# Joining the half-empty row tails of two batches in the second product of an attention and MLP kernel, with fewer buffers elsewhere

## The chip, the cores and the metric

The kernel runs on one core of one Trainium2 chip. The metric is the device time of one execution in microseconds (us), as a median of several.

Names: PE (TensorE) does the matmuls, PEld its weight loads, DVE (VectorE) and ACT (ScalarE) move and transform results, POOL issues the loads with a type cast, SP issues the stores. "L406" is line 406 of that version's file. Line numbers shift from version to version; tile names do not, except that `ch1T` is called `ch1Tp` after the change.

## The reference

```python
# q, k, v: (8 batches, 8 heads, 576 rows, 64); causal attention with a window of 64
x = softmax(mask(q @ k.T / 8)) @ v            # heads joined: (8, 576, 512)
u = x + ((x.transpose(0, 2, 1) @ U) @ V).transpose(0, 2, 1)      # U, V: rank 32
out = u + relu(u @ w_ch1) @ w_ch2             # w_ch1: 512x2048, w_ch2: 2048x512
```

A batch has 576 rows: four chunks of 128 and a tail of 64.

## The kernel before

The kernel interleaves two jobs: the MLP of batch b and the attention of batch b+1. The attention needs `v` in two alignments: `vaugA` is loaded, and `vaugB` is the same data moved by 64 rows, which DVE copies from `vaugA`. The kernel is written with a layer that orders each engine's instructions itself, allots buffers and sets all semaphores. The order on an engine is therefore not simply that of the source, and the number of buffers helps to decide it.

```python
ld_pool  = tc.tile_pool(name="ld",  bufs=3)      # q, k
va_pool  = tc.tile_pool(name="va",  bufs=3)      # vaugA and vaugB: three buffers each
ch1_pool = tc.tile_pool(name="ch1", bufs=1)
out_pool = tc.tile_pool(name="osb", bufs=6)
ps_big   = tc.tile_pool(name="ps_big", bufs=2, space=PSUM)   # shared by psA, psU, pshh
# ...
        vaugB = va_pool.tile([P, NFULL, H, VW], BF16, name="vaugB")
        def prep():
            nc.vector.memset(vaugA[:, :, :, D:VW], 1.0)
            nc.vector.tensor_copy(out=vaugB[0:W, 0:NFULL, :, :], in_=vaugA[W:P, 0:NFULL, :, :])
            nc.vector.tensor_copy(out=vaugB[W:P, 0:NFULL, :, :], in_=vaugA[0:W, 1:NC, :, :])
# ... the second product, one chunk t of rows
        def make_ch2(t):
            def f():
                mt = P if t < NFULL else REM          # 128, and 64 for the tail
                psU = ps_big.tile([P, 512], FP32, name="psU", tag="big")
                for i in range(NFC):                  # 16
                    nc.tensor.matmul(psU[0:mt, :], ch1T[:, i, t * P : t * P + mt], w2b[:, i, :],
                                     start=(i == 0), stop=(i == NFC - 1))
                osb = out_pool.tile([P, DM], FP32, name="osb")
                nc.vector.tensor_tensor(out=osb[0:mt, :], in0=psU[0:mt, :],
                                        in1=u_b16[0:mt, t, :], op=ALU.add)
                nc.sync.dma_start(out=out[b, t * P : t * P + mt, :], in_=osb[0:mt, :])
# ... the main loop
    for b in range(B):
        if b + 2 < B:
            loads(b + 2)
        mlp = mlp_phases(b, holders.pop(b))
        # emit_interleaved(attention of b + 1, mlp of b); the last batch has its MLP alone
```

The softmax here doesn't subtract the row's maximum and nothing guards it: scores larger than these inputs give would overflow.

## Time and profile before

| | before |
|---|---|
| median time | 435.55 us (434.36 to 436.71, 6 runs) |
| span of the profiled run | 433.6 us |
| PE busy | 88% of the span |
| second product (psU) in the chain of waits | 30% of the span |

The page first: the busy shares, and the TensorE clock that was granted, in tenths, over 40 equal slices.

```profile
PE 383.1 (88%) x3034; PEld 199.1 (46%) x3088; DVE 229.2 (53%) x622; ACT 137.1 (32%) x361; POOL 109.5 (25%) x134
...
PEclk9965897999996999989999999999999999999999
```

PE is the busiest engine by far (88%, the next 53%) and holds 67% of the chain of waits, so what lengthens PE's work, or stops it, costs time. The clock row shows dips below 9 in the first 45% of the span and none later. Something happens there that later batches do not have.

To find it, read the chain that ended last in order of time and pick a fixed point of each batch: the start of its third full chunk of psU. The columns are start, length, what, and how many.

```profile
88.13 3.40 PE psU L406 x15
92.09 7.02 PE psU L406 x32
...
140.28 3.40 PE psU L406 x15
...
192.09 3.40 PE psU L406 x15
...
243.18 3.40 PE psU L406 x15
...
290.57 3.45 PE psU L406 x16
...
338.02 3.45 PE psU L406 x16
...
385.47 3.45 PE psU L406 x16
```

The differences are 52.15, 51.81, 51.09, 47.39, 47.45 and 47.45 us. The same work takes about 4.3 us longer in the first three. (The line at 92.09 us is the fourth full chunk and the tail of batch 0 together.) The VectorE timeline of the first slow batch shows why: start, length, instruction, and in brackets how long the engine sat idle before it and what ended that.

```profile
125.06 0.42 DVE L282 TENSOR_TENSOR x_b<-xr,rcp 64x256 bf16<-64x256 f32 x1
130.41 0.76 DVE L164 COPY vaugB<-vaugA 64x2304 bf16<-64x2304 bf16 x1 [4.93 <-DMA vaugA<-in_v_dram]
131.19 0.69 DVE L414 TENSOR_TENSOR osb<-psU,u_b 128x512 f32<-128x512 f32 x1
```

The copy at 130.41 us is for batch 5, whose attention is three batches ahead. With three `vaugB` buffers there is a free one, so the copy stands in DVE's queue just behind the load that it needs, and DVE waits for the transfer. The urgent instruction, `osb`, which empties a PSUM buffer that PE needs, stands behind the copy. In this trace DVE ran nothing past the waiting copy: psU was complete at about 128.6 us, and `osb` starts only at 131.19 us, right behind the copy. The next two batches show the same order (copies at 183.01 and 234.10 us after 5.39 and 4.67 us of idle time, `osb` at 183.79 and 234.88 us). PE's timeline and its clock in the same stretch (columns of the second fence: stretch, its length, busy us of each engine, granted clock, DMA share, GB/s):

```profile
128.42 0.38 PE L318 MATMUL psA<-hhTb,vmoe 128*128 128x512 bf16 x1
131.94 1.18 PE L318 MATMUL psA<-hhTb,vmoe 128*128 128x512 bf16 x2 [3.14 <-DVE osb L414]
```

```profile
124.00:129.00 5.00, 4.62 (x23) 1.86 (x24) 1.36 (x6) 0.58 (x1) 3.21 (x4) 1.00 1.60 105
129.00:134.00 5.00, 2.05 (x7) 0.71 (x6) 3.41 (x6) 0.00 (x0) 0.00 (x0) 0.72 0.40 69
134.00:139.00 5.00, 5.00 (x17) 1.94 (x17) 2.05 (x3) 0.00 (x0) 0.00 (x0) 0.60 0.00 0
139.00:144.00 5.00, 4.95 (x33) 2.64 (x33) 0.97 (x2) 1.31 (x5) 0.00 (x0) 1.00 0.14 52
```

PE stands still for 3.14 us and then runs at a mean granted clock of 0.60 from 134 to 139 us: the chunk of 16 psU matmuls that starts at 134.78 us takes 5.2 us, where the 16 at 290.57 us, in a batch without a stall, take 3.45. The stall is paid twice. Its sums over the whole kernel, in the view of waits (us in total, times, longest):

```profile
DVE vaugB L164 <- DMA vaugA<-in_v_dram: 23.3, 7, 5.4
...
PE psA L318 <- DVE osb L414: 11.9, 7, 3.6
...
PE psB L382 <- DVE x_b L282: 3.5, 1, 3.5
```

The last line belongs to the first batch. There the copy stands ahead of an attention result (`x_b`) instead of `osb`, and PE waits for that; after this wait its granted clock is 0.50 from 71 to 76 us:

```profile
68.47 0.76 DVE L164 COPY vaugB<-vaugA 64x2304 bf16<-64x2304 bf16 x1 [3.51 <-DMA vaugA<-in_v_dram]
```

The other two stalls show it too: after PE gaps of 3.60 and 2.88 us the granted clock is 0.50 from 186 to 188 us and from 237 to 240 us. From 255 us to the end, where no wait of PE is longer than 0.6 us, its mean is 1.00. Beyond this sequence, nothing here shows what ties the clock to the gap.

### The profile page before, as it was taken

What the parts mean: (1) busy time and instruction counts of PE and PEld (TensorE: products, weight loads), DVE (VectorE), ACT (ScalarE), POOL (GpSimd) and SP (SyncE); (2) the same over time, 40 slices, a digit from 0 to 9 for tenths busy, and PEclk for the clock granted to TensorE, in tenths of its full rate; (3) what the DMA queues carried; (4) which work ended last, traced back from release to release, by engine and by line L of the source; (5) the groups of instructions that cost most, each with busy time, mean ns of one, the idle gap of its engine ahead of it and who ended that gap; (6) DMA issues with size and microseconds to landing.
All of it is one profiled execution on the core that took longest, in us unless ns stands there. A gap on an engine that the chain in (4) does not pass through costs nothing.

```text
span 433.6 us, 7457 instructions
## 1 busy us (share of the span) xinstructions
PE 383.1 (88%) x3034; PEld 199.1 (46%) x3088; DVE 229.2 (53%) x622; ACT 137.1 (32%) x361; POOL 109.5 (25%) x134
## 2 busy tenths in 40 slices
PE   0647996899988999699996999999998999999996
PEld 0433652346533565245642455445643465444542
DVE  5376774636745187443775257642775167532321
ACT  1331751026510174113720236212830255221300
POOL 9929459933430052300703000000000000000000
PEclk9965897999996999989999999999999999999999
DMA  8999999994980179811949110011000110011011
GB/s 56 147 194 137 178 153 135 153 139 58 91 56 24 73 60 64 57 48 60 80 33 80 48 39 2 2 48 49 13 2 26 49 39 2 2 48 62 0 50 61
DMA packets 121042, 28.35 MB, mean 65 GB/s; under 512 B 113808, under 2 KB 115888, under 8 KB 121008
## 3 DMA queue, kind: packets, MB, share of 16 engines
q0 software_dynamic: 115760, 18.43, 57.4%
q1 hardware_dynamic: 5248, 9.44, 6.1%
q8 instruction: 24, 0.39, 0.4%
q14 instruction: 10, 0.08, 0.1%
HBM read 36.85 MB, written 9.44 MB: 107 GB/s over the span
## 4 chain that ended last, share of the span: by engine, by line
PE 67%; DMA 12%; POOL 8%; DVE 5%; ACT 5%; issue 2%; DVEq 0%; POOLq 0%
PE psU L406 30%; PE psA L374 19%; DMA vaugA<-in_v_dram 5%; POOL vaugA L143 4%; DMA w2b<-in_moe_w_ch_dram 4%; PE xr L273 3%; DMA w1b<-in_moe_w_ch_dram 3%; PE psB L382 3%; ACT ptj L236 3%; PE sc L228 3%; DVE u_b L325 2%; POOL qb L137 2%; POOL kb L133 2%; PE tp L191 2%; PE tp L340 2%
## 5 line engine op out<-in xcount | busy, mean ns | idle before, releaser
L406 PE MATMUL psU<-w2b,ch1T 128*128 128x512 bf16 (+1 forms) x628 | 148.2, 387 | 1.0 <-DVE ch1T L393 0.5
L374 PE MATMUL psA<-uT,w1b 128*128 128x512 bf16 x474 | 134.0, 383 | 2.4 <-ACT uT L348 0.6
L406 PEld LDWEIGHTS <-ch1T 128*128 128x128 bf16 (+1 forms) x640 | 63.1, 102 | 72.9 <-issue 11.0
L414 DVE TENSOR_TENSOR osb<-psU,u_b 128x512 f32<-128x512 f32 (+1 forms) x40 | 27.6, 690 | 107.1 <-PE psU L406 107.0
L390 ACT ACTIVATE ch1T<-psA 128x512 bf16<-128x512 f32 x64 | 38.2, 597 | 65.2 <-PE psA L374 61.0
L133 POOL DMA_DIRECT2D kb<-in_k_dram x40 | 36.9, 923 | 81.2 <-PE tp L178 72.3
L374 PEld LDWEIGHTS <-w1b 128*128 128x128 bf16 x512 | 42.3, 98 | 23.0 <-issue 0.8
L393 DVE TENSOR_SCALAR ch1T<-psA 128x512 bf16<-128x512 f32 x64 | 44.1, 689 | 13.3 <-PE psA L374 10.1
L348 ACT COPY uT<-tp 128x512 bf16<-128x512 bf16 x32 | 19.0, 594 | 94.6 <-PE tp L343 94.6
L236 ACT ACTIVATE ptj<-sc 128x384 bf16<-128x384 f32 x96 | 43.9, 495 | 6.6 <-PE sc L228 4.9
L382 PEld LDWEIGHTS <-w1b 128*128 128x128 bf16 x512 | 31.2, 99 | 24.8 <-DVE x_b L282 4.0
L143 POOL DMA_DIRECT2D vaugA<-in_v_dram x40 | 33.8, 886 | 30.2 <-PE psA L374 30.2
L382 PE MATMUL psB<-uT,w1b 128*128 128x64 bf16 x512 | 37.0, 195 | 4.6 <-DVE x_b L282 3.5
L137 POOL DMA_DIRECT2D qb<-in_q_dram x40 | 36.2, 904 | 9.6 <-DMA w2b<-in_moe_w_ch_dram 9.6
L183 ACT COPY kt<-tp 128x512 bf16<-128x512 bf16 x32 | 18.8, 588 | 58.6 <-PE tp L178 58.5
L242 DVE TENSOR_TENSOR ptj<-ptj,maskall 128x384 bf16<-128x384 bf16 x96 | 31.3, 353 | 10.5 <-ACT ptj L236 9.2
L203 DVE COPY qbd<-tp 64x512 bf16<-64x512 bf16 x64 | 26.9, 421 | 17.1 <-PE tp L196 16.4
L282 DVE TENSOR_TENSOR x_b<-xr,rcp 128x256 bf16<-128x256 f32 (+1 forms) x80 | 32.9, 415 | 1.4
L273 PEld LDWEIGHTS <-ptj 128*64 128x64 bf16 x576 | 18.3, 116 | 30.8 <-DVE x_b L282 13.9
L228 PE MATMUL sc<-qbd,kt 128*128 128x128 bf16 x288 | 29.4, 224 | 3.4 <-DVE qbd L203 1.5
L318 PE MATMUL psA<-hhTb,vmoe 128*128 128x512 bf16 (+1 forms) x40 | 17.7, 447 | 15.4 <-DVE osb L414 11.9
L228 PEld LDWEIGHTS <-kt 128*128 128x128 bf16 x288 | 20.7, 100 | 14.0 <-issue 8.5
(48 smaller groups left out, 295.0 us busy)
## 6 DMA issues: line engine op xcount, KB each, us to landing
out_dram<-osb SPq DMA_DIRECT2D x32, 256.0 KB, 2.0
kb<-in_k_dram POOLq DMA_DIRECT2D x32, 128.0 KB, 4.5
qb<-in_q_dram POOLq DMA_DIRECT2D x32, 128.0 KB, 4.6
vaugA<-in_v_dram POOLq DMA_DIRECT2D x32, 128.0 KB, 4.5
w1b<-in_moe_w_ch_dram POOLq DMA_DIRECT2D x1, 2048.0 KB, 14.4
w2b<-in_moe_w_ch_dram POOLq DMA_DIRECT2D x1, 2048.0 KB, 16.9
out_dram<-osb SPq DMA_DIRECT2D x8, 128.0 KB, 2.2
kb<-in_k_dram POOLq DMA_DIRECT2D x8, 64.0 KB, 4.0
```

The lines of the kernel that those rows point to most:

```text
L133: nc.gpsimd.dma_start(out=kb16[0:rows, c, :, :], in_=k[b, :, c * P : c * P + rows, :].rearrange("h p d -> p h d"),)
L137: nc.gpsimd.dma_start(out=qb16[0:rows, c, :, :], in_=q[b, :, c * P : c * P + rows, :].rearrange("h p d -> p h d"),)
L143: nc.gpsimd.dma_start(out=vaugA[0:rows, c, :, 0:D], in_=v[b, :, c * P : c * P + rows, :].rearrange("h p d -> p h d"),)
L228: nc.tensor.matmul(sc[:, bb, :], kt[:, j, w0 : w0 + P], qbd[:, j, blk, :, :].rearrange("p g q -> p (g q)"), start=True, stop=True,)
L236: nc.scalar.activation(out=ptj[:, prange, :, :], in_=sc[:], func=ACT.Exp, scale=scale,)
L273: nc.tensor.matmul(xr[r0 : r0 + W, hl, 0 : D + 1], pts[j][:, blk, g, :], rhs, start=True, stop=True,)
L282: nc.vector.tensor_tensor(out=x_b16[0:mt, t, 4 * hh : 4 * hh + 4, :], in0=xr[0:mt, :, 0:D], in1=rcp[0:mt, :, :].to_broadcast([mt, 4, D]), ...
L374: nc.tensor.matmul(psA[:, :], w1b[:, dc, i * P : (i + 1) * P], uT[:, dc, 0:512], start=(dc == 0), stop=(dc == NDC - 1),)
L382: nc.tensor.matmul(psB[:, :], w1b[:, dc, i * P : (i + 1) * P], uT[:, dc, 512:S], start=(dc == 0), stop=(dc == NDC - 1),)
L390: nc.scalar.activation(out=ch1T[:, i, 0:512], in_=psA[:, :], func=ACT.Relu)
L393: nc.vector.tensor_relu(out=ch1T[:, i, 0:512], in_=psA[:, :])
L406: nc.tensor.matmul(psU[0:mt, :], ch1T[:, i, t * P : t * P + mt], w2b[:, i, :], start=(i == 0), stop=(i == NFC - 1),)
```

## The change

The intent: the tail of a batch fills 64 of the 128 rows of a psU result, yet its 16 matmuls take as long as those of a full chunk (a full chunk and a tail take 7.02 us, a full chunk alone 3.45). The change keeps the first layer's results of two batches in one tile, places the two tails side by side, and computes both with one chunk of 128 rows when the odd batch is done. It also takes buffers away elsewhere, presumably to make room for the doubled tile. From the shapes, `ch1Tp` takes 36 KB per partition instead of 18 KB; the buffers given up are two of 5 KB (q, k), one `vaugA` of 5.6 KB, two `vaugB` of 4.5 KB and two `osb` of 2 KB.

```diff
-    ld_pool = ...(name="ld", bufs=3)
-    va_pool = ...(name="va", bufs=3)
+    ld_pool = ...(name="ld", bufs=2)
+    va_pool = ...(name="va", bufs=2)
+    ut_pool = ...(name="ut", bufs=2)
+    vb_pool = ...(name="vb", bufs=1)
-    out_pool = ...(name="osb", bufs=6)
+    out_pool = ...(name="osb", bufs=4)
-        vaugB = va_pool.tile(...)
+        vaugB = vb_pool.tile(...)
-        ch1T = ch1_pool.tile([P, NFC, S], BF16, name="ch1T")
+        even = b % 2 == 0
+        if even:
+            ch1Tp = ch1_pool.tile([P, NFC, 2 * S], BF16, name="ch1Tp")
+            colb, colt = 0, 512              # columns of the chunks, and of the tail
+            utail = ut_pool.tile([P, DM], BF16, name="utail")
+            nc.scalar.copy(out=utail[0:REM, :], in_=u_b16[0:REM, NFULL, :])
+        else:                                # same ch1Tp and utail as the even batch
+            colb, colt = S + REM, S          # this tail stands next to the even one's
+            nc.scalar.copy(out=utail[REM:P, :], in_=u_b16[0:REM, NFULL, :])
         # ... the first layer writes ch1Tp at colb and colt
+        # chunks of an even batch: its four full ones. Of an odd batch: its four full ones,
+        # then one of 128 rows at column 512 (both tails), residual utail, two stores
-                nc.sync.dma_start(out=out[b, t * P : t * P + mt, :], in_=osb[0:mt, :])
+                for (bb, s0, s1), orows in stores:
+                    nc.sync.dma_start(out=out[bb, s0:s1, :], in_=osb[orows, :])
```

More of the change, by code (lines that the diff above doesn't have):

```diff
@@ L52 @@
     qbd_pool = ctx.enter_context(tc.tile_pool(name="qbd", bufs=1))
-    ld_pool = ctx.enter_context(tc.tile_pool(name="ld", bufs=3))
-    va_pool = ctx.enter_context(tc.tile_pool(name="va", bufs=3))
+    ld_pool = ctx.enter_context(tc.tile_pool(name="ld", bufs=2))
+    va_pool = ctx.enter_context(tc.tile_pool(name="va", bufs=2))
+    ut_pool = ctx.enter_context(tc.tile_pool(name="ut", bufs=2))
+    vb_pool = ctx.enter_context(tc.tile_pool(name="vb", bufs=1))
     kt_pool = ctx.enter_context(tc.tile_pool(name="kt", bufs=2))
@@ L59 @@
     wk_pool = ctx.enter_context(tc.tile_pool(name="wk", bufs=4))
-    out_pool = ctx.enter_context(tc.tile_pool(name="osb", bufs=6))
+    out_pool = ctx.enter_context(tc.tile_pool(name="osb", bufs=4))
     ps_sc = ctx.enter_context(tc.tile_pool(name="ps_sc", bufs=2, space=bass.MemoryType.PSUM))
@@ L125 @@
     loaded = {}
+    pair_state = {}
     def loads(b):
@@ L159, in attention_phases @@
         kt = kt_pool.tile([P, HP, S], BF16, name="kt")
-        vaugB = va_pool.tile([P, NFULL, H, VW], BF16, name="vaugB")
+        vaugB = vb_pool.tile([P, NFULL, H, VW], BF16, name="vaugB")
         def prep():
@@ L366, in mlp_phases @@
         phases = []
-        ch1T = ch1_pool.tile([P, NFC, S], BF16, name="ch1T")
+        even = b % 2 == 0
+        partner_missing = even and (b + 1 >= B)
+        if even:
+            ch1Tp = ch1_pool.tile([P, NFC, 2 * S], BF16, name="ch1Tp")
+            pair_state["tile"] = ch1Tp
+            pair_state["u_even"] = u_b16
+            colb = 0
+            colt = 512
+            utail = ut_pool.tile([P, DM], BF16, name="utail")
+            pair_state["utail"] = utail
+            nc.scalar.copy(out=utail[0:REM, :], in_=u_b16[0:REM, NFULL, :])
+        else:
+            ch1Tp = pair_state["tile"]
+            colb = S + REM
+            colt = S
+            utail = pair_state["utail"]
+            nc.scalar.copy(out=utail[REM:P, :], in_=u_b16[0:REM, NFULL, :])
         def make_ch1(i):
@@ L389, in f @@
                 if i % 2 == 0:
-                    nc.scalar.activation(out=ch1T[:, i, 0:512], in_=psA[:, :], func=ACT.Relu)
-                    nc.scalar.activation(out=ch1T[:, i, 512:S], in_=psB[:, :], func=ACT.Relu)
-                else:
-                    nc.vector.tensor_relu(out=ch1T[:, i, 0:512], in_=psA[:, :])
-                    nc.vector.tensor_relu(out=ch1T[:, i, 512:S], in_=psB[:, :])
+                    nc.scalar.activation(
+                        out=ch1Tp[:, i, colb : colb + 512], in_=psA[:, :], func=ACT.Relu
+                    )
+                    nc.scalar.activation(
+                        out=ch1Tp[:, i, colt : colt + REM], in_=psB[:, :], func=ACT.Relu
+                    )
+                else:
+                    nc.vector.tensor_relu(out=ch1Tp[:, i, colb : colb + 512], in_=psA[:, :])
+                    nc.vector.tensor_relu(out=ch1Tp[:, i, colt : colt + REM], in_=psB[:, :])
             return f
@@ L399, in mlp_phases, with make_ch2 @@
             phases.append(make_ch1(i))
-        def make_ch2(t):
+        if even:
+            chunks = []
+            for t in range(NFULL):
+                chunks.append(
+                    (
+                        P * t,
+                        [(slice(0, P), u_b16[:, t, :], slice(0, P))],
+                        [((b, P * t, P * t + P), slice(0, P))],
+                    )
+                )
+            if partner_missing:
+                chunks.append(
+                    (
+                        NFULL * P,
+                        [(slice(0, REM), u_b16[0:REM, NFULL, :], slice(0, REM))],
+                        [((b, NFULL * P, S), slice(0, REM))],
+                    )
+                )
+        else:
+            chunks = []
+            for t in range(NFULL):
+                chunks.append(
+                    (
+                        S + REM + P * t,
+                        [(slice(0, P), u_b16[:, t, :], slice(0, P))],
+                        [((b, P * t, P * t + P), slice(0, P))],
+                    )
+                )
+            chunks.append(
+                (
+                    NFULL * P,
+                    [(slice(0, P), utail[:, :], slice(0, P))],
+                    [((b - 1, NFULL * P, S), slice(0, REM)), ((b, NFULL * P, S), slice(REM, P))],
+                )
+            )
+        def make_ch2(cidx):
+            col0, resid, stores = chunks[cidx]
+            tail_direct = partner_missing and col0 == NFULL * P
+            nrows = REM if tail_direct else P
             def f():
-                mt = P if t < NFULL else REM
                 psU = ps_big.tile([P, 512], FP32, name="psU", tag="big")
@@ L406, in f @@
                     nc.tensor.matmul(
-                        psU[0:mt, :],
-                        ch1T[:, i, t * P : t * P + mt],
+                        psU[0:nrows, :],
+                        ch1Tp[:, i, col0 : col0 + nrows],
                         w2b[:, i, :],
@@ L413, in f @@
                 osb = out_pool.tile([P, DM], FP32, name="osb")
-                nc.vector.tensor_tensor(
-                    out=osb[0:mt, :],
-                    in0=psU[0:mt, :],
-                    in1=u_b16[0:mt, t, :],
-                    op=ALU.add,
-                )
-                nc.sync.dma_start(out=out[b, t * P : t * P + mt, :], in_=osb[0:mt, :])
-            return f
-        for t in range(NC):
-            phases.append(make_ch2(t))
+                for orows, uap, prows in resid:
+                    nc.vector.tensor_tensor(
+                        out=osb[orows, :],
+                        in0=psU[prows, :],
+                        in1=uap,
+                        op=ALU.add,
+                    )
+                for (bb, s0, s1), orows in stores:
+                    nc.sync.dma_start(out=out[bb, s0:s1, :], in_=osb[orows, :])
+            return f
+        for cidx in range(len(chunks)):
+            phases.append(make_ch2(cidx))
         return phases
```

## The prediction

> **What bounds it now.** TensorE. The page gives PE 88% of 433.6 us; in the chain of waits PE holds 67%, second-product matmuls (psU) alone 30%. From one batch's last 32 psU matmuls to the next's, that chain shows 47.45 us for the last three steady batches, but 52.15, 51.81 and 51.08 for the three before. Those carry a stall: in the VectorE timeline the vaugB copy (three buffers) runs up to three batches ahead of its use and waits 4.7 to 5.4 us for a vaugA transfer issued moments earlier. The osb eviction queued behind it is late, and TensorE waits 2.9 to 3.6 us for its PSUM bank (waits of PE: psA <- osb). The granted clock then falls to 0.6 (stretch 134 to 139 us) and 16 psU matmuls take 5.0 us, not 3.5. [...] The first batch has the same stall: PE waits 3.46 us at 67 to 71 us, then runs at clock 0.50.
>
> **What the change does.**
> 1. Removes four of eight tail chunks: 64 of 640 psU matmuls. A tail uses 64 of 128 output rows, but its matmuls still stream 512 columns: 32 psU matmuls, half of them tail, take 7.02 us in the chain, 3.51 per chunk. On the PE-bound path: 4 x 3.5 = -14.0 us. Four osb adds (0.68 us each) go too, off the path.
> 2. Cuts vaugB to one buffer and vaugA, kb, qb to two. By the instruction order each vaugB copy now stands behind the previous batch's last attention product and serves the very next batch, whose vaugA was loaded a batch earlier. The head-of-line stall should vanish: (52.15+51.81+51.08) - 3 x 47.45 = -12.7 us; in the first batch stall (3.5 us) and cold clock (some 2.5 us): about -6 us. This bundled part is worth more than the stated intent. Loads wait for earlier buffers, but lead their use by about 40 us against 10 us of transfer.
> 3. Adds eight 64-row ScalarE copies (estimate 0.5 us each, from the 0.58 us of uT copies) and later vaugB copies (2 x 0.75 us), which fit in the 3 us VectorE idles before osb. ScalarE is 32% busy. Cost: 0 to 3 us in all.
> 4. The joined ch1 tile stays single-buffered; TensorE's order already separates old reads from new writes. The last batch keeps five chunks, so the end is unchanged.
>
> **Sum.** 435.5 - 14.0 - 12.7 - 6.0 + about 1 = about 404 us; range 398 to 411. Chances: faster by over 2% 0.97, within 2% 0.02, slower by over 2% 0.01.
>
> **What would show the steps right.** psU matmuls 576, not 640. The chain's batch intervals alternate about 44 (even batch) and 47.5 us. VectorE's wait for vaugA transfers falls from 23.3 us to under 4, PE's wait psA <- osb from 11.9 to about 4; no clock slice under 0.9 after 60 us. Batches with loads in flight are as fast as those without.
>
> **What would make it wrong.** If loads, now spread over more batches, arrive late, the stall returns, each about 4.5 us. If the vaugB copy, now between the last x_b operations, delays pshh, PE waits about 0.8 us more per batch. If the first vaugB copy still waits for its load, the 6 us stays. If intervals alternate but shrink little, the matmuls were not the bound. If only step 1 holds, the time is about 421 us.

The "cold clock (some 2.5 us)" in the -6.0 is an estimate; the 5 us from 71 to 76 us at a granted clock of 0.50 give 2.5 us. The lead of 40 us and the 10 us of transfer are estimates as well; for what was measured see "Loads would be early enough" below.

## The result, and the profile after

The changed kernel takes 403.78 us in the median (402.83 to 404.84, 8 runs), against 435.29 us before (16 runs in all). The ratio is 0.9277, with a 95% interval of 0.9258 to 0.9295. (A ratio is the mean time of one kernel's runs over that of the other's of the same rounds, so it is not quite the ratio of the medians quoted.) The profiled run has a span of 401.9 us.

The same views as before, first the page:

```profile
PE 360.1 (90%) x2969; PEld 190.0 (47%) x3024; DVE 227.5 (57%) x618; ACT 141.8 (35%) x369; POOL 111.3 (28%) x134
...
PEclk9975699999999999999999999999999999999999
```

Weight loads fell from 3088 to 3024, which is the 64 matmuls taken out. (Of the matmul records themselves a few are missing from both traces: 628 of 640 psU are there before, 562 of 576 after.) After the start the clock row has no dip any more; from 60 us to the end the mean granted clock is 1.00. The chain, at the same point of each batch:

```profile
82.41 3.40 PE psU L468 x15
...
126.42 3.40 PE psU L468 x15
...
173.83 3.45 PE psU L468 x16
...
217.85 3.45 PE psU L468 x16
...
265.31 2.59 PE psU L468 x12
...
309.13 2.37 PE psU L468 x11
...
356.40 3.45 PE psU L468 x16
```

The intervals alternate: 44.01, 47.41, 44.02, 47.46, 43.82 and 47.27 us. An interval that begins in an even batch lacks a tail and is about 3.5 us shorter. One that begins in an odd batch is as long as an undisturbed batch was before (47.45 us), although loads are in flight in two of the three. The VectorE timeline at the end of an attention, and the waits:

```profile
115.69 1.18 DVE L167 COPY vaugB<-vaugA 64x2304 bf16<-64x2304 bf16 x1
116.90 0.42 DVE L285 TENSOR_TENSOR x_b<-xr,rcp 64x256 bf16<-64x256 f32 x1
117.35 0.75 DVE L168 COPY vaugB<-vaugA 64x2304 bf16<-64x2304 bf16 x1
119.40 0.69 DVE L477 TENSOR_TENSOR osb<-psU,u_b 128x512 f32<-128x512 f32 x1 [1.30 <-PE psU L468]
```

```profile
DVE vaugB L167 <- DMA vaugA<-in_v_dram: 1.7, 2, 1.1
...
PE psA L321 <- DVE osb L477: 4.0, 7, 0.6
```

The copies stand in the same place of the stream, but now they serve the next batch, whose `vaugA` was loaded one batch earlier. Nothing is waited for, and `osb` follows at once when psU is complete. What is left of PE's wait is at most 0.6 us a time.

Where the 31.7 us between the two spans came from, read off the two chains:

| stretch | before | after | difference |
|---|---|---|---|
| start to the third chunk of batch 0 | 88.13 | 82.41 | -5.7 |
| from there to the third chunk of batch 6 | 297.34 | 273.99 | -23.4 |
| from there to the end | 48.13 | 45.50 | -2.6 |

The middle row holds three removed tails (3 x 3.5 = 10.5 us) and three stalls (12.7 us by the intervals before). The last row holds one removed tail, less something; see the sixth experiment.

### The profile page after: what moved, and what is told of

Its sections match the earlier page's. It is cut to its first block, busy times and chain, and to the rows that moved or that the text cites. A ratio compares the mean times of both kernels' runs of the same rounds, so it can differ in the third digit from the quotient of the medians.

```text
span 401.9 us, 7328 instructions
## 1 busy us (share of the span) xinstructions
PE 360.1 (90%) x2969; PEld 190.0 (47%) x3024; DVE 227.5 (57%) x618; ACT 141.8 (35%) x369; POOL 111.3 (28%) x134
## 4 chain that ended last, share of the span: by engine, by line
PE 73%; DVE 7%; ACT 7%; DMA 5%; POOL 5%; issue 2%; DVEq 0%; POOLq 0%
PE psU L468 30%; PE psA L393 23%; PE xr L276 4%; ACT ptj L239 4%; PE psB L401 4%; DMA w1b<-in_moe_w_ch_dram 4%; DVE u_b L328 3%; PE sc L231 3%; PE tp L194 2%; ACT ch1Tp L409 2%; PE tp L176 2%; PE tp L343 2%; PE pshh L304 2%; POOL kb L136 1%; DVE osb L477 1%
## 5 line engine op out<-in xcount | busy, mean ns | idle before, releaser
L468 PE MATMUL psU<-w2b,ch1Tp 128*128 128x512 bf16 x562 | 130.0, 379 | 1.2 <-DVE ch1Tp L416 0.4
L468 PEld LDWEIGHTS <-ch1Tp 128*128 128x128 bf16 x576 | 54.7, 98 | 62.7 <-issue 2.8
L477 DVE TENSOR_TENSOR osb<-psU,u_b 128x512 f32<-128x512 f32 x32 | 22.1, 692 | 88.0 <-PE psU L468 88.0
L409 ACT ACTIVATE ch1Tp<-psA 128x512 bf16<-128x512 f32 x64 | 38.2, 597 | 61.4 <-PE psA L393 57.9
L416 DVE TENSOR_SCALAR ch1Tp<-psA 128x512 bf16<-128x512 f32 x64 | 44.1, 689 | 12.7 <-PE psA L393 8.5
L146 POOL DMA_DIRECT2D vaugA<-in_v_dram x40 | 35.9, 931 | 40.6 <-PE psA L393 40.3
L245 DVE TENSOR_TENSOR ptj<-ptj,maskall 128x384 bf16<-128x384 bf16 x96 | 31.3, 353 | 10.5 <-ACT ptj L239 9.2
L284 DVE RECIPROCAL rcp<-xr 128x4 f32<-128x4 f32 (+1 forms) x80 | 14.1, 179 | 22.4 <-PE xr L276 22.2
## 6 DMA issues: line engine op xcount, KB each, us to landing
w2b<-in_moe_w_ch_dram POOLq DMA_DIRECT2D x1, 2048.0 KB, 17.1
```

Source lines behind the costliest of these rows:

```text
L146: nc.gpsimd.dma_start(out=vaugA[0:rows, c, :, 0:D], in_=v[b, :, c * P : c * P + rows, :].rearrange("h p d -> p h d"),)
L409: nc.scalar.activation(out=ch1Tp[:, i, colb : colb + 512], in_=psA[:, :], func=ACT.Relu)
L416: nc.vector.tensor_relu(out=ch1Tp[:, i, colb : colb + 512], in_=psA[:, :])
L468: nc.tensor.matmul(psU[0:nrows, :], ch1Tp[:, i, col0 : col0 + nrows], w2b[:, i, :], start=(i == 0), stop=(i == NFC - 1),)
```

## The experiments

The question was not whether the kernel is faster, but which part of the change does it. Theory A: pairing is worth its 64 matmuls, and more than half of the gain comes from the smaller number of `vaugB` buffers, which moves the copy in DVE's queue. Rival B: the loads were spread over more batches by the two-deep buffers, and that removed the stall. Rival C: the joined tile frees the border between batches. The first four runs shared one set of runs of the kernel before (434.77 us), the last three another (434.69 us). All seven gave correct results.

**1. Only vaugB in a single buffer** (the kernel before, with this edit alone):

```diff
+    vb_pool = ...(name="vb", bufs=1)
-        vaugB = va_pool.tile(...)
+        vaugB = vb_pool.tile(...)
```

> The kernel before with one thing changed: vaugB gets a pool of its own with one buffer (three before); no pairing, loads three deep. Theory A (the stall comes from where the vaugB copy stands in VectorE's queue, which its buffer count decides): the stalls go, 435.3 - 12.7 - 6.0 = about 417 us, PE's wait psA <- osb falls from 11.9 to about 4 us. Rival B (the stall went because q, k, v loads are spread over more batches): about 435 us, unchanged. Rival C (the joined ch1 tile is needed to free the batch border): about 435 us.

Measured: 417.34 us, ratio 0.9596 (0.9554 to 0.9637). Its waits:

```profile
PE psA L319 <- DVE osb L415: 4.0, 7, 0.6
```

```profile
DVE vaugB L165 <- DMA vaugA<-in_v_dram: 1.2, 1, 1.2
```

Taking two buffers away, and nothing else, gives 17.4 us. Loads are still three deep and there is no joined tile, so neither B nor C is needed for this part. The wait for PSUM is 4.0 us, the same as in the changed kernel.

**2. Only the loads two deep** (q, k, vaugA in two buffers; vaugB still in three):

```diff
-    ld_pool = ...(name="ld", bufs=3)
-    va_pool = ...(name="va", bufs=3)
+    ld_pool = ...(name="ld", bufs=2)
+    va_pool = ...(name="va", bufs=2)
+    vb_pool = ...(name="vb", bufs=3)
```

> The kernel before with q, k and vaugA two deep instead of three, vaugB still three deep. By the instruction order the vaugB copies still stand right behind the load of their own vaugA. Theory A: the stall stays and now meets four steady batches (loads 4 to 7), not three, and the first: 435.3 + 4.3 = about 440 us. Rival B (shallower, spread loads remove it): about 417 us.

Measured: 439.01 us, ratio 1.0093 (1.0047 to 1.0139). Its waits:

```profile
PE psA L319 <- DVE osb L415: 14.0, 7, 3.4
```

```profile
DVE vaugB L165 <- DMA vaugA<-in_v_dram: 22.7, 6, 5.2
```

The other half of the buffer change, alone, makes the kernel slightly slower (with an interval clear of 1), as theory A said: with a load in flight in one more batch, one more batch stalls. In its chain four intervals are long (52.39, 51.56, 51.13 and 51.12 us) instead of three. Rival B falls.

**3. All the new buffer counts, no pairing** (edits 1 and 2 with vaugB in one buffer, and osb in four):

> The kernel before with every buffer count of the changed kernel (q, k, vaugA two, vaugB one, osb four) and no pairing. Theory A: about 417 us, as with vaugB alone, so that pairing alone is worth 417 - 404 = 13 to 14 us. Rival C (joined tile does more than remove matmuls): above 421 us, so that pairing is worth more than its 14 us of matmuls.

Measured: 417.63 us, ratio 0.9599 (0.9555 to 0.9644), the same as experiment 1. What the changed kernel has beyond this one is the pairing alone: 417.63 - 403.78 = 13.9 us between medians. That is the 4 x 3.5 us of the removed matmuls, and leaves nothing for rival C that can be told from noise.

**4. The changed kernel with a second vaugB buffer:**

```diff
-    vb_pool = ...(name="vb", bufs=1)
+    vb_pool = ...(name="vb", bufs=2)
```

> The changed kernel with two vaugB buffers instead of one, all else as changed. By the instruction order the copies for batches 4 to 7 again stand right behind their own loads. Theory A: the stall returns in the first batch (6 us) and in four steady ones (4.3 us each): about 403.8 + 6 + 17 = 427 us, slower although it has more memory. Rivals B and C: about 404 us.

Measured: 423.97 us, ratio 0.9739 (0.9687 to 0.9792). One buffer more costs 20 us. VectorE's timeline, PE's timeline, and the waits of DVE and of PE, show the old stall again:

```profile
124.44 0.41 DVE L285 TENSOR_TENSOR x_b<-xr,rcp 64x256 bf16<-64x256 f32 x1
129.36 0.76 DVE L167 COPY vaugB<-vaugA 64x2304 bf16<-64x2304 bf16 x1 [4.51 <-DMA vaugA<-in_v_dram]
```

```profile
130.89 1.18 PE L321 MATMUL psA<-hhTb,vmoe 128*128 128x512 bf16 x2 [2.72 <-DVE osb L477]
```

```profile
DVE vaugB L167 <- DMA vaugA<-in_v_dram: 24.5, 7, 4.8
```

```profile
PE psA L321 <- DVE osb L477: 12.8, 7, 3.0
...
PE xr L276 <- DVE x_b L285: 6.0, 2, 5.2
```

This agrees with theory A in kind, and was 3 us below its number. Against the changed kernel, its four stalled intervals are longer by 2.8, 3.2, 3.5 and 3.5 us (expected 4.3), and the first batch by 8.7 us (expected 6); there PE waits 5.2 us. Why the steady stalls are shorter is not shown.

What no run tests is the order alone: three `vaugB` buffers with the copy moved by hand behind `osb`. That the order is how the buffer count acts is read from the timelines, in which `osb` starts right behind the late copy.

The last three runs try to improve on the changed kernel.

**5. U and V ahead of the big weight load.** In the start, TensorE waits 4.06 us for the small `U`, which stands behind the 2 MB load of `w1b`.

```diff
     def load_weights1():
-        nc.gpsimd.dma_start(out=w1b[:], in_=moe_w_ch1...)
         # ... the loads of U and V
+        nc.gpsimd.dma_start(out=w1b[:], in_=moe_w_ch1...)
```

> The changed kernel with the small U and V loads issued ahead of the 2 MB w1b load. TensorE waits 4.06 us at 29 to 33 us for the U load, which lands with w1b. If nothing else binds there: about 4 us less, 400 us. If w1b (first needed at 43.9 us) or the second batch's loads bind instead: 0 to 2 us less.

Measured: 401.56 us, ratio 0.9236 (0.9208 to 0.9264), against 0.9277 (0.9258 to 0.9295) for the changed kernel. These intervals overlap a little; but experiment 6, which ran in the same call and takes as long as the changed kernel, gave 403.21 to 403.86 us, against 401.29 to 401.67 here. The wait for U is gone, yet 2.2 us come of it, not 4. The chain of this run now goes, at that time, through the second batch's `vaugA`:

```profile
37.98 5.60 DMA vaugA<-in_v_dram
```

So the loads of the next batch took over a part, as the expectation allowed.

**6. The joined tail first in the last batch.** The changed kernel ends with two stores of 128 KB in one queue.

```diff
+        if b == B - 1 and not even:
+            chunks.insert(0, chunks.pop())
```

> The changed kernel, in the last batch the joined tail chunk is emitted first, so that the last chunk ends in one 256 KB store instead of two 128 KB stores in one queue. The time from the last psU matmul to the end is 5.1 us in the changed kernel (396.8 to 401.9) and 4.0 us before. If the second store is what costs it: 0.5 to 1.1 us less, about 403 us. If not: no change.

Measured: 403.49 us, ratio 0.9281 (0.9253 to 0.931). In time this is no difference that can be told from noise. The last row of each of the three timelines is the final `osb` (before, changed, this run):

```profile
429.71 0.68 DVE L414 TENSOR_TENSOR osb<-psU,u_b 64x512 f32<-64x512 f32 x1 [2.88 <-PE psU L406]
```

```profile
396.90 0.69 DVE L477 TENSOR_TENSOR osb<-psU,utail 128x512 f32<-128x512 f32 x1 [2.82 <-PE psU L468]
```

```profile
397.36 0.69 DVE L477 TENSOR_TENSOR osb<-psU,u_b 128x512 f32<-128x512 f32 x1 [2.76 <-PE psU L468]
```

From the start of that instruction to the end of the span it is 3.9 us before (433.6), 5.0 us in the changed kernel (401.9) and 4.1 us here (401.5). So the second store does cost about 1 us in these profiles. But in this run the first batch came 0.6 us later (third chunk at 82.97 us), and the medians do not resolve the rest. It stays an observation from one profile each.

**7. Both, and the mask selections behind the first loads.** Three POOL instructions that build the mask (2.6 us) stood between the first q and k loads; here they follow them.

> The changed kernel with the tail chunk first in the last batch, U and V loads first, and the three mask selections on POOL (2.6 us) moved behind the first batch's q and k loads, which they delay. Expected: the two gains above added, and up to 2.6 us more from earlier transposes at the start: 396 to 400 us.

Measured: 399.00 us, ratio 0.9188 (0.9156 to 0.9221). This version is the fastest of all: 4.8 us below the changed kernel. No run has the mask move alone, so its share is not measured by itself. The third chunk of batch 0 starts at 78.76 us, against 80.51 in experiment 5 and 82.41 in the changed kernel. The start is the one part where PE still waits long for loads: in the changed kernel up to 5.0 us (for `kb`), with no PE wait over 0.6 us after the first 60 us; in this run up to 4.8 us.

## Why the prediction was right

The forecast was 404 us, and 403.78 us was measured. Its terms, one by one:

- **The removed matmuls, -14.0 us.** Right: experiment 3 puts pairing alone at 13.9 us, and the chain's intervals of even batches fell to about 44 us. In these traces a psU matmul takes the same time whether 64 or 128 of the result rows are used: the trace before had 32 of them, half of them tails, in 7.02 us (219 ns each), and 16 full ones in 3.45 us (216 ns each), both at a granted clock of 1.00. The view by form lists the tails as `128*64 128x512` (mean of one record 380 ns; the records overlap) and the full ones as `128*128 128x512` (388 ns).
- **The stalls, -12.7 and about -6 us.** Right: experiment 1 gives 17.4 us for the one edit that moves the copy, against 18.7 forecast. The start became 5.7 us shorter, against 6. The waits fell as forecast (1.7 us against "under 4"; 4.0 us against "about 4").
- **Loads would be early enough.** Right. The vaugA load issued at 113.6 us is copied at 163.2 us, a lead of some 45 us after the 4.7 us of its issue. In the trace before, the four vaugA loads that DVE waited for at the stalls took 7.1 to 8.3 us from the first issue to the start of the copy.
- **Added copies cost 0 to 3 us.** Right in size. In experiment 3, the four intervals in which the first copy runs while POOL issues a `vaugA` load, and takes 1.18 us, are 47.6 us. The one whose copy meets no load (0.76 us) is 47.4, and so is the one without a copy. So 0.2 us per batch goes with the meeting of copy and load issue, and the moved copy alone costs nothing that can be seen. What makes the copy longer is not isolated: in the changed kernel the first copy takes 1.18 us inside a vaugA issue (113.64 to 118.38 us), but the second, at 117.35 us inside the same one, takes 0.75 us. The eight ScalarE copies took 0.62 us each (0.5 was the estimate), and nothing is seen to wait for them.
- **"The end is unchanged".** Not quite: two stores in place of one lengthen the end by about 1 us in the profile. It is within the stated range and was not in the sum.

That the sum came out within 0.3 us is in part luck. By the chains, the stretch between the third chunks lost 23.4 us, where three tails and three stalls make 23.2. The start gave 0.3 us less than forecast and the last row 0.9 us less, and the 1 us set aside for the copies happens to cover both. The mechanism and the two large terms are not luck; experiments 1 and 3 measured them apart.

The prediction got the larger half of the gain from a part of the change that its intent does not name. What made this possible was to compare batches that do the same work, and to look at the order of instructions on DVE before and after.

## What to carry to other kernels

A buffer more is not always better: here a second `vaugB` buffer raised the changed kernel from 403.78 to 423.97 us. Where a layer orders the queues, a free buffer can let a prefetch copy be placed ahead of urgent work. In the kernel before, DVE then waited for a transfer that nobody needed yet (4.93 us at 125 us), and ran the urgent work only behind the copy. When equal stages differ in time, look at the first instruction that waits and at what stands behind it in the same queue. And when a change bundles its idea with buffer counts, run the counts alone first: here they were worth more (17.1 us) than the idea (13.9 us).
